# A top-k attention and a two-layer MLP on one core: where the halves, the mask's operands, the values' products and the turned weights' transfers stand

## The chip, the core and the metric

The kernel runs on one core of a Trainium2 chip. The core has a TensorE (PE, matrix products, with a queue for weight loads, PEld), a VectorE (DVE), a ScalarE (ACT), a GpSimd (POOL) and a SyncE (SP), whose queue issues nearly all transfers here. Each engine runs its own instructions in the order in which the program wrote them, and engines wait for each other through semaphores. The metric is the device time of one execution in microseconds (us); less is better.

## The reference

Attention with a hard top-k mask, followed by a block with a layer norm, two weight matrices and a residual:

```python
# q, k, v: (8 batches, 8 heads, 576 rows, 64)
scores = scale * np.matmul(q, k.transpose(0, 1, 3, 2))
kth = np.partition(scores, -32, axis=-1)[..., -32:-31]
scores = np.where(scores >= kth, scores, -1e9)
scores = scores - np.max(scores, axis=-1, keepdims=True)
attn = np.exp(scores)
attn = attn / (np.sum(attn, axis=-1, keepdims=True) + 1e-09)
attn_out = np.matmul(attn, v)
x = attn_out.transpose(0, 2, 1, 3).reshape(8, 576, 512)
xn = (x - mean(x)) / np.sqrt(var(x) + 1e-06) * g_ln
out = x + np.maximum(xn @ w_ch1, 0.0) @ w_ch2   # 512 -> 2048 -> 512
```

q, k, v and g_ln arrive as float32, and all arithmetic is float32; the two weight matrices come as 64-bit numbers, which the kernel turns into float32 itself in its first steps (`Piece`).

## The kernel before, in words

**Units, groups, jobs.** A *unit* is 128 query rows of both heads of a head pair: two score tiles of 128 x 576. The 576 rows of a batch make four such units (qt 0 to 3) and a *rest* unit, whose single tile holds the last 64 rows of both heads. A batch has four head pairs, so 20 units, and the whole run has 160. Two or three units of one head pair make a *group*, which is also a *job* here: [0, 1], [2, 3] and [rest] in batch 0, [0, 1] and [2, 3, rest] in batch 1, [0, 1, rest] and [2, 3] from batch 2 on. The four head pairs of one kind of group come one after another.

**Steps.** The main loop (L1170) goes through steps n = 0, 1, 2, ... and in each step writes the instructions of several units in different stages, so that all engines have work. In step n, apart from the first eight units:

- unit n+2: `scores` (L366): TensorE's products, copied by ScalarE into a tile `sc` (a pool of 5 buffers);
- unit n+1 (`nxt`): `halve` (L400, called at L1233, between the second and the third quarter of unit n's selection): VectorE takes the larger and the smaller of each two columns into `hi` (2 buffers) and `lo` (1 buffer);
- unit n (`u`): `select` in four parts (L415, called at L1199, L1228, L1264, L1298): VectorE finds eight largest at a time (MAX8) and strikes them out (MATCH_REPLACE8). The first eight stay in `u.top`, the last eight in `u.thr`, whose column 7 is the threshold;
- unit n-1 (`mk`): `prepare` (L442, called at L1209): GpSimd first runs `watch` (L452), which notes from `hi` whether the halving may have lost a value, then makes the two operands of the mask, `edge` and `bias`, in spare columns of `u.thr`. Later in the step `mask` (L483, called at L1254 and L1282): a Relu on ScalarE and a subtraction on GpSimd for each tile, into `e` (2 buffers). For the first 18 units (`CONVERTING`) VectorE runs `watch` and makes both operands at the end of the unit's own step (L1300);
- unit n-2 (`ex`): `weigh` (L491): ScalarE's Exp with its row sums. Then the weights have to be turned, so that keys lie along partitions, into the group's tile `pt` (1 buffer): either by TensorE and ScalarE (`turn`, L542: four transposes and one copy for each tile, and a transpose and a copy for the last columns), or, for a *moved* unit, by VectorE (`move`, L523: 32 x 32 blocks are turned in place in `sc`, the tile goes to memory in one transfer, L534, and comes back in four, L537), while the last columns still go through TensorE (`parts[-1]`, L1280). Moved are the units from batch 2 on that aren't rest units and aren't the last of their group: 72;
- the group whose last unit is n-3: `values` (L600, called at L1197): TensorE's products of V with `pt`, and one product with the tile `ends` for the last keys; `take_values` (L618), then `place` (L630) turns the result back and scales it.

**V's tile.** `load_values` (L305) brings V of a head pair by SP; it is written near the end of the step after the job's last unit (L1286). `fill_ends` (L311) copies two corners of it into the single tile `ends` on GpSimd; it is written in the middle of the next step (L1251), ahead of `mask`.

**The first eight units** (`EARLY`) run a step closer: mask and weights of unit n-1 and values of n-2 in step n, beside the conversion of the weight matrices.

**The block.** When four head pairs have given their part of two row tiles, a block of 256 rows is queued (`give`, L1121): mean and variance on VectorE, the transposes, 64 products with w_ch1 and 56 with w_ch2 (seven products of halves instead of eight, with sums on GpSimd, L818). `fill` (L263), called eight times in each step, puts a planned share of these products between the attention's instructions on TensorE, and runs the actions that were put off by a number of such calls (`Later`, L237). What is left after the last step (`END`, L1014) is run off at the end (L1317).

The kernel is written out twice; the second copy runs only where `watch` has found a doubt, and doesn't run here. In all stages SP's transfers stand in the order of the text: a transfer that waits holds up all that is written after it on SP.

Of the kernel before, what the change touches and what calls it, by code (L numbers as in the profile page):

```python
# [10 lines left out]
ALU = mybir.AluOpType  # L11
# [8 lines left out]
STEEP = 2.0**90  # L20
# [9 lines left out]
def compute(  # L30
# [229 lines left out]

    loads = Later()

    def fill(least=0):  # L263
        tick[0] += 1
        loads.settle(LOAD_AGE)
        ends_later.settle(END_AGE)
        fetch_forms(FETCH_AGE)
        owed[0] = min(owed[0] + share[0], 6.0)
        while todo and (not todo[0][3] or todo[0][3]()):
            if owed[0] < todo[0][1] / 2 and least <= 0:  # L270
                break
            least -= 1
            pop()
# [168 lines left out]
    def prepare(u):  # L442

        nt = len(u.tiles)
        u.bias, u.edge = u.thr[:, 0:nt, 5], u.thr[:, 0:nt, 6]
        if doubt is not None:
            watch(u)
        eng = nc.vector if u.i < CONVERTING else nc.gpsimd
        eng.tensor_scalar(u.edge, u.thr[:, 0:nt, 7], STEEP, 0.0, ALU.mult, ALU.add)  # L449
        eng.tensor_scalar(u.bias, u.top[:, 0:nt, 0], -scale, 0.0, ALU.mult, ALU.add)  # L450

    def watch(u):  # L452

        nt = len(u.tiles)
        c = 1 + 2 * (u.i % 16)
        eng = nc.vector if u.i < CONVERTING else nc.gpsimd
        eng.tensor_tensor(  # L457
            watched[:, c : c + nt], u.hi[:, 0:nt, HALF + 7], u.thr[:, 0:nt, 7], ALU.subtract
        )
        if u.i % 16 == 15 or u.i == N - 1:  # L460
            u.ends_watch = True
# [61 lines left out]
    def move(u):  # L523

        i0 = place_of(u)
        ni = P // 32
        blocks = u.sc[:].rearrange("p t n -> p (t n)")[:, 0 : 2 * JP]
        for t in range(2):
            nc.vector.transpose(
                blocks.rearrange("p (j t c n) -> p j t c n", j=ni, t=2, c=J)[:, :, t],  # L530
                u.e[:, t, t * R : t * R + JP].rearrange("p (c j k) -> p j c k", c=J, k=32),
            )
        hbm = hbmpool.tile([P, 2 * JP], FP32, tag="turned", name="turned")
        nc.sync.dma_start(hbm[:], blocks)  # L534
        for j in range(ni):
            to = u.group.pt[j * 32 : (j + 1) * 32, 0 : 2 * J].rearrange("k c n -> k (c n)")
            nc.sync.dma_start(  # L537
                to[:, i0 * 2 * P : (i0 + ni) * 2 * P].rearrange("k (i x) -> k i x", i=ni),
                hbm[:, j * 2 * P : (j + 1) * 2 * P].rearrange("(i k) x -> k i x", k=32),
            )  # L540

# [393 lines left out]
    PER_ROW = 1.71e-3  # L935
    SUM_AGE, END_AGE, FETCH_AGE, STORE_AGE, LOAD_AGE = 7, 6, 10, 8, 3
    blocks = []
    plain_done, formed, used, fetched = [None], [None], [], [0]
# [74 lines left out]
    N = len(units)  # L1013
    END = N + 6  # L1014

# [11 lines left out]

    for u in units[jobs[5 * NHP].first :]:
        u.moved = not u.rest and u is not u.group.units[-1]


    full = slice(0, P)
# [10 lines left out]
    for j in jobs:  # L1043
        if j.hp == NHP - 1:
            b = j.b
            step = j.last + (3 if j.last < EARLY else 4)
            tiles = [(b, qt) for g in j.groups for qt in g.qts if qt < J]
# [24 lines left out]
    def at(i):  # L1072
        return units[i] if 0 <= i < N else None

    def after(n):

        turned = at(n - 1) if n - 1 < EARLY else at(n - 2) if n - 2 >= EARLY else None
        last = at(n - 2) if n - 2 < EARLY else at(n - 3) if n - 3 >= EARLY else None
        return turned, last.group if last and last is last.group.units[-1] else None

# [89 lines left out]
    for n in range(END):  # L1170
# [12 lines left out]
        late = late if late and late.rest and late.job.b % 2 else None  # L1183
        parts = turn(ex) if ex else []
        early = ex is not None and n - 1 < EARLY
# [10 lines left out]
        if g:  # L1196
            values(g)  # L1197
        if u:
            select(u, 0)  # L1199
# [5 lines left out]
        if n == gives_first:  # L1205
            for blk, i in rows_of.pop(n):
                blk.stats(i)
        if mk and mk.i >= CONVERTING:
            prepare(mk)  # L1209
        if early:  # L1210
            for t in range(2):
                mask(ex, t)
            for t in range(2):
                weigh(ex, t)
# [6 lines left out]
        if g:  # L1221
            take_values(g)
        if parts and not moved:
            parts[0]()
# [4 lines left out]
        for x in batches.get(n - 1, []):  # L1229

            x.shift()
        if nxt:
            halve(nxt)  # L1233
        sums_later.settle(SUM_AGE)
# [13 lines left out]
        if not quick:  # L1248
            weights(n, 1)
        if n in ends_due:  # L1250
            fill_ends(ends_due.pop(n))  # L1251
        fill()
        if mk and not early:
            mask(mk, 0)  # L1254
        if g:
# [27 lines left out]
        fill()  # L1283
        for x in (u if n < EARLY else None, mk if n > EARLY else None):
            if x and x is units[x.job.last]:
                load_values(x.job)  # L1286
                ends_due[n + 1] = x.job
        if quick:
# [8 lines left out]
        if u:  # L1297
            select(u, 3)  # L1298
            if u.i < CONVERTING:
                prepare(u)  # L1300
        for x in (g, quick):
# [73 lines left out]
```

## Time and profile before

| | us |
|---|---|
| median of 3 runs | 1684.97 (1684.85 to 1687.71) |
| the profiled execution | 1683.85 |
| its span, first to last instruction | 1682.1 |
| busy: TensorE / VectorE / GpSimd / ScalarE | 1517.3 / 1339.3 / 1118.3 / 1067.6 |
| mean granted TensorE clock | 0.959 of full speed |
| products of the block with w_ch1 (L750) | 2304 instructions, two for each float32 product |
| products of the block with w_ch2 (L907, L789) | 1904 and 64 instructions |
| mask subtraction on GpSimd (L489) | 288 instructions, 1428 ns each |
| halves on VectorE (L412, L413) | 160 of each, 778 and 743 ns each |
| blocks turned by VectorE (L529) | 144 instructions, 685 ns each |

Busy time is the time in which an engine's profiled instructions run; an engine's idle time before an instruction is put down to what released it. A matmul's end is modelled, and matmuls overlap, so TensorE's busy share is an upper bound of its use.

### The profile page before, as it was taken

To read this page: it belongs to the slowest core of one execution; us is meant where nothing else is said; L and a number is where in the kernel's file an instruction comes from. 1 tells how busy PE (TensorE), PEld (TensorE's weight loads), DVE (VectorE), ACT (ScalarE), POOL (GpSimd) and SP (SyncE) were. 2 spreads that over 40 slices of the span, in tenths; PEclk is the share of its full clock that TensorE was granted. 3 is DMA by queue.
4 is the path that set the end of the run, shared out by engine and by line. 5 is a ranking of instruction groups with operands and counts; after the bars stand their busy time and mean duration, and the time that the engine had idled before them with its cause. 6 is when DMAs were issued, how large, how long until landed. Compare 5 with 4: busy or idle time off the path is not lost. (4 is left out here: it accounts for less than half of the span.)

```text
span 1682.1 us, 27351 instructions
## 1 busy us (share of the span) xinstructions
PE 1517.3 (90%) x7898; PEld 1137.5 (68%) x7898; DVE 1339.3 (80%) x3990; ACT 1067.6 (63%) x2712; POOL 1118.3 (66%) x1742
## 2 busy tenths in 40 slices
PE   3557889999979998999899999999999999999997
PEld 1335546677656676667677777677677776778886
DVE  5999988788879988899889988799889988884000
ACT  6777856677656766667566765676556765754411
POOL 4667967967556675668576866676657775757433
PEclk9768999999989999999999999999999999999999
DMA  6523334411455445544555444545555455442211
GB/s 177 151 86 129 117 75 118 119 44 46 109 150 170 116 124 146 153 143 125 161 156 160 127 136 135 157 130 134 158 147 164 123 140 167 146 129 86 85 35 52
DMA packets 355687, 211.51 MB, mean 126 GB/s; under 512 B 247492, under 2 KB 327880, under 8 KB 355528
## 3 DMA queue, kind: packets, MB, share of 16 engines
q1 hardware_dynamic: 350792, 209.08, 43.4%
q8 instruction: 65, 1.06, 0.3%
q10 hardware_dynamic: 4736, 0.59, 0.2%
q14 instruction: 94, 0.77, 0.1%
HBM read 145.62 MB, written 63.96 MB: 125 GB/s over the span
## 5 line engine op out<-in xcount | busy, mean ns | idle before, releaser
L750 PE MATMUL hps<-xT,w 128*128 128x256 f32 x2304 | 548.5, 383 | 2.4 <-ACT xT L712 2.4
L489 POOL TENSOR_TENSOR e<-e,sc 128x576 f32<-128x576 f32 x288 | 408.6, 1428 | 178.6 <-ACT e L486 149.5
L750 PEld LDWEIGHTS hps<-xT,w 128*128 128x128 f32 x2304 | 421.9, 191 | 72.9 <-issue 14.9
L434 DVE MAX8 m<-hi 128x8 f32<-128x296 f32 (+1 forms) x1152 | 458.2, 444 | 0.2
L420 DVE MATCH_REPLACE8 hi<-m,hi 128x288 f32<-128x288 f32 (+1 forms) x864 | 378.5, 444 | 0.0
L497 ACT ACTIVATE e<-e,m 128x576 f32<-128x576 f32 x288 | 225.0, 781 | 185.0 <-POOL e L489 184.6
L907 PE MATMUL ops<-w,h 128*128 128x256 f32 x1360 | 325.1, 381 | 0.0
L907 PEld LDWEIGHTS ops<-w,h 128*128 128x128 f32 x1360 | 247.6, 190 | 40.4 <-issue 7.7
L412 DVE TENSOR_TENSOR hi<-sc 128x576 f32<-128x576 f32 (+1 forms) x160 | 124.5, 778 | 183.5 <-POOL watched L457 178.4
L486 ACT ACTIVATE e<-sc,m 128x576 f32<-128x576 f32 x288 | 224.3, 782 | 13.5 <-POOL m L449 12.5
L372 ACT COPY sc<-scps 128x288 f32<-128x288 f32 x576 | 193.0, 406 | 38.0 <-PE scps L391 18.8
L605 PE MATMUL av<-pt,vb 128*64 128x256 f32 (+2 forms) x1088 | 164.4, 450 | 49.7 <-DMA qin<-in_q_dram 24.4
L314 POOL COPY ends<-vb 64x64 f32<-64x64 f32 x136 | 34.0, 250 | 219.1 <-DMA vb<-in_v_dram 180.9
L605 PEld LDWEIGHTS av<-pt,vb 128*64 128x64 f32 x1088 | 84.4, 154 | 121.0 <-issue 84.2
L773 ACT ACTIVATE h<-hps 128x512 f32<-128x512 f32 x144 | 86.5, 600 | 91.9 <-PE hps L750 90.9
L391 PE MATMUL scps<-kT,late_qT 64*128 64x288 f32 (+3 forms) x832 | 128.1, 415 | 6.2 <-ACT pt L563 5.5
L907 PE MATMUL ops<-wt,s 128*128 128x256 f32 x544 | 129.2, 381 | 0.0
L551 PE MATMUL tp<-ident,e 128*128 128x128 f32 x576 | 94.9, 291 | 38.1 <-ACT e L497 37.9
L551 PEld LDWEIGHTS tp<-ident,e 128*128 128x128 f32 x576 | 74.3, 149 | 66.5 <-ACT e L497 51.6
L413 DVE TENSOR_TENSOR lo<-sc 128x576 f32<-128x576 f32 (+1 forms) x160 | 118.9, 743 | 0.0
L391 PE MATMUL scps<-kT,qT 64*128 64x288 f32 x512 | 94.3, 469 | 26.9 <-ACT sign L167 11.8
L426 DVE MAX8 hi<-lo 128x8 f32<-128x288 f32 x288 | 118.1, 446 | 0.0
(107 smaller groups left out, 1998.4 us busy)
## 6 DMA issues: line engine op xcount, KB each, us to landing
turned<-sc SPq DMA_DIRECT2D x72, 512.0 KB, 2.6
pt<-turned SPq DMA_DIRECT2D x288, 128.0 KB, 2.8
w<-forms SPq DMA_DIRECT2D x136, 256.0 KB, 4.1
vb<-in_v_dram SPq DMA_DIRECT2D x68, 288.0 KB, 3.9
raw<-in_moe_w_ch_dram SPq DMA_DIRECT2D x32, 512.0 KB, 3.7
kT<-kept SPq DMA_DIRECT2D x36, 288.0 KB, 3.5
kin<-in_k_dram SPq DMA_DIRECT2D x128, 72.0 KB, 2.4
kept<-kT SPq DMA_DIRECT2D x32, 288.0 KB, 3.2
```

What stands on the lines that cost most here:

```text
L372: nc.scalar.copy(u.sc[:, t, s * HALF : (s + 1) * HALF], made[s][t][:, 0:HALF])
L391: nc.tensor.matmul(ps[i * R : i * R + ql, o : o + width], qT[r, q0 : q0 + ql], kT[r, k0 : k0 + width], start=True, stop=True,)
L412: nc.vector.tensor_tensor(hi, a, b, ALU.max)
L420: nc.vector.match_replace(x, m[:, t, :], x, LOWEST)
L434: nc.vector.max(m[:, t, :], u.hi[:, t, 0:width])
L486: nc.scalar.activation(u.e[:, t], u.sc[:, t], AF.Relu, bias=u.edge[:, t : t + 1], scale=-STEEP)
L489: nc.gpsimd.tensor_tensor(u.e[:, t], u.e[:, t], u.sc[:, t], ALU.subtract)
L497: nc.scalar.activation(u.e[:, t], u.e[:, t], AF.Exp, bias=u.bias[:, t : t + 1], scale=-scale, accum_out=g.den[:, col : col + 1],)
L551: nc.tensor.transpose(ps[:, c * P : (c + 1) * P], u.e[:, t, c * P + t * R : (c + 1) * P + t * R], ident[:],)
L605: nc.tensor.matmul(av[h * D : (h + 1) * D, 0 : g.nq], vb[:, h * (J + 1) + c, :], g.blocks[:, h, 0 : g.nq // 32, c, :], start=(c == 0), sto ...
L750: nc.tensor.matmul(ps[0][:, side * N : (side + 1) * N], w1[:, c, f * P : (f + 1) * P], self.xT[:, c, 0:N], start=(c == 0), stop=(c == NC - 1),
L907: nc.tensor.matmul(bank[name][:, 0:Q], a(j), rhs, start=first and j == 0, stop=(j == G - 1), skip_group_check=not first,)
```

## The change

The halves of the next unit go from the middle of the step to its end. `prepare` runs on ScalarE for all units, in place in columns of `u.top` and `u.thr`, right ahead of the mask; `watch` runs on GpSimd for all units, early in the step. A group's products with V come two, three or four steps after its last unit (`lag`): four where the next job's first unit is moved. `move` only turns the blocks in its own step; the transfer to memory is written two `fill` calls later (`SEND_AGE`), and the four transfers back, with the turn of the last columns, are written one step later, behind the products with V. Moved are now the units from the second kind of group of batch 0 on (`units[EARLY:]`), 88 in all. `load_values` and `fill_ends` change places within the step. `END` grows by one step, and so do the steps at which blocks are given behind a lag of four.

```diff
@@ fill
+        sends.settle(SEND_AGE)
         ends_later.settle(END_AGE)
@@ prepare, watch
-        u.bias, u.edge = u.thr[:, 0:nt, 5], u.thr[:, 0:nt, 6]
-        if doubt is not None:
-            watch(u)
-        eng = nc.vector if u.i < CONVERTING else nc.gpsimd
-        eng.tensor_scalar(u.edge, u.thr[:, 0:nt, 7], STEEP, 0.0, ALU.mult, ALU.add)
-        eng.tensor_scalar(u.bias, u.top[:, 0:nt, 0], -scale, 0.0, ALU.mult, ALU.add)
+        u.bias, u.edge = u.top[:, 0:nt, 0], u.thr[:, 0:nt, 7]
+        nc.scalar.mul(u.edge, u.edge, STEEP)
+        nc.scalar.mul(u.bias, u.bias, -scale)
...
-        eng = nc.vector if u.i < CONVERTING else nc.gpsimd
-        eng.tensor_tensor(
+        nc.gpsimd.tensor_tensor(
@@ move
-        nc.sync.dma_start(hbm[:], blocks)
-        for j in range(ni):
-            to = ...
-            nc.sync.dma_start(...)
+
+        def bring():
+            i0 = place_of(u)
+            for j in range(ni):
+                to = ...
+                nc.sync.dma_start(...)
+
+        sends.add(lambda: nc.sync.dma_start(hbm[:], blocks))
+        brings[u.i + 3] = bring
@@ the plan
+    SEND_AGE = 2
-    END = N + 6
+    END = N + 7
-    for u in units[jobs[5 * NHP].first :]:
+    for u in units[EARLY:]:
         u.moved = not u.rest and u is not u.group.units[-1]
+    for j, after_j in zip(jobs, jobs[1:] + [None]):
+        waits = after_j is not None and units[after_j.first].moved
+        j.groups[0].lag = 2 if j.last < EARLY else 4 if waits else 3
-            step = j.last + (3 if j.last < EARLY else 4)
+            step = j.last + 1 + j.groups[0].lag
@@ after(n): the group whose lag is reached at step n
-        last = at(n - 2) if n - 2 < EARLY else at(n - 3) if n - 3 >= EARLY else None
-        return turned, last.group if last and last is last.group.units[-1] else None
+        for age in (2, 3, 4):
+            last = at(n - age)
+            if last and last is last.group.units[-1] and last.group.lag == age:
+                return turned, last.group
+        return turned, None
@@ the step
-        parts = turn(ex) if ex else []
+        parts = turn(ex) if ex and not ex.moved else []
...
         if g:
             values(g)
+        if n in brings:
+            brings.pop(n)()
+            turn(at(n - 3))[-1]()
         if u:
             select(u, 0)
...
-        if mk and mk.i >= CONVERTING:
-            prepare(mk)
+        if mk and doubt is not None:
+            watch(mk)
         if early:
+            prepare(ex)
...
-        if nxt:
-            halve(nxt)
         sums_later.settle(SUM_AGE)
...
             weights(n, 1)
-        if n in ends_due:
-            fill_ends(ends_due.pop(n))
+        for x in (u if n < EARLY else None, mk if n > EARLY else None):
+            if x and x is units[x.job.last]:
+                load_values(x.job)
+                ends_due[n + 1] = x.job
         fill()
         if mk and not early:
+            prepare(mk)
             mask(mk, 0)
...
             mask(mk, 1)
         fill()
-        for x in (u if n < EARLY else None, mk if n > EARLY else None):
-            if x and x is units[x.job.last]:
-                load_values(x.job)
-                ends_due[n + 1] = x.job
+        if n in ends_due:
+            fill_ends(ends_due.pop(n))
...
             select(u, 3)
-            if u.i < CONVERTING:
-                prepare(u)
+        if nxt:
+            halve(nxt)
```

## The prediction

> **What bounds the kernel now.** I read the table of busy times by stretch first, with the run cut where the halve of units 20, 40, ... 140 starts and where the last unit's does: nine stages, the first with the conversion of the weights, the last (147.3 us) with no selection left. Columns: length, then busy time (and instructions) of PE, PEld, DVE, ACT and POOL, then the granted clock.
>
> ```profile
> 0.00:239.90 239.90, 154.51 (x660) 94.99 (x661) 205.57 (x547) 178.05 (x403) 166.22 (x163) 0.85 0.43 123
> 239.90:413.60 173.70, 166.47 (x948) 119.80 (x948) 148.33 (x467) 127.06 (x330) 132.51 (x203) 0.97 0.33 87
> 413.60:597.50 183.90, 164.40 (x861) 119.99 (x856) 160.82 (x487) 118.85 (x314) 117.96 (x196) 0.94 0.46 131
> 597.50:784.00 186.50, 170.08 (x906) 128.17 (x905) 164.57 (x500) 119.20 (x316) 124.20 (x205) 0.97 0.50 143
> 784.00:969.50 185.50, 179.29 (x962) 137.37 (x961) 163.51 (x493) 121.43 (x318) 130.32 (x218) 0.99 0.50 144
> 969.50:1159.20 189.70, 181.87 (x972) 138.89 (x971) 163.16 (x495) 122.61 (x327) 128.60 (x217) 0.98 0.51 145
> 1159.20:1345.70 186.50, 179.18 (x959) 136.87 (x958) 163.06 (x492) 121.13 (x315) 123.30 (x204) 0.98 0.49 142
> 1345.70:1534.80 189.10, 184.80 (x980) 143.63 (x980) 154.60 (x469) 118.80 (x306) 124.53 (x205) 0.99 0.46 134
> ```
>
> No engine is full in stages 2 to 4: TensorE and VectorE both stand some 10% of the time. In stages 5 to 8 TensorE is recorded busy 96 to 98%, but that count is generous: matmul ends are modelled. What TensorE needs I count instead. In the timeline sixteen block products in a row take 3.62 us, one ending 0.38 after its start: 0.216 us from start to start. The rest of a stage of 20 units is about 56 us: scores 20 x 1.15 (8 matmuls 1.24 us), 8 groups' products with V at 2.7 (16 take 2.37, the two with ends 0.6 to 0.8), about 112 transposes at 0.109 (four in 0.60 with one tail). Stages 5 to 8 hold 546, 548, 537 and 585 block products (L750 and L907 asked for by stretch), so need 118 + 56 = 174, 174, 172 and 180 us; stages 3 and 4 with 438 and 487 need 151 and 161; stage 2, with 364, 28 long ones at 0.43 and 194 transposes, 155. All lie below the lengths.
>
> The waits say who holds whom (total, times, longest):
>
> ```profile
> ACT e L497 <- POOL e L489: 184.6, 93, 9.4
> POOL ends L314 <- DMA vb<-in_v_dram: 180.9, 38, 11.9
> DVE hi L412 <- POOL watched L457: 178.4, 71, 11.4
> ...
> PE av L605 <- DMA qin<-in_q_dram: 24.4, 6, 5.8
> ...
> SPq L534 <- DVE m L434: 423.7, 71, 14.3
> SPq L537 <- DMA turned<-sc: 175.9, 72, 5.3
> ```
>
> The second line is the root of the first and third, as one place in the timeline shows:
>
> ```profile
> 1239.94 0.50 SPq L309 DMA_DIRECT2D vb<-in_v_dram  x1
> ...
> 1244.59 0.52 POOL L314 COPY ends<-vb 64x64 f32<-64x64 f32 x2 [7.59 <-DMA vb<-in_v_dram]
> ...
> 1244.73 2.37 PE L605 MATMUL av<-pt,vb 128*64 128x320 f32 x16 [2.90 <-issue]
> ...
> 1246.64 0.78 ACT L497 ACTIVATE e<-e,m 128x576 f32<-128x576 f32 x1 [5.62 <-POOL e L489]
> ...
> 1248.17 0.76 DVE L412 TENSOR_TENSOR hi<-sc 128x576 f32<-128x576 f32 x1 [5.93 <-POOL watched L457]
> ```
>
> V's load stands on SP behind the sending of the turned weights, which waits for VectorE, and the bringing back, which waits for the sending to land. It is issued late, GpSimd stands 7.59 us in fill_ends, and behind it in GpSimd's queue are the mask's subtraction (ScalarE's Exp waits) and the next watch, which frees the buffer that halve wants (VectorE waits 5.93).
>
> **The change, part by part.**
>
> *Load and corners of V.* The load is written half a step earlier, ahead of the next sending, the copy half a step later: some 4 us each at 9.3 us a step, against a landing of 3.9 (median). The 180.9 us on GpSimd should go, and with them most of VectorE's 178.4. Late next: fill_ends now stands behind the previous group's products with V in the same step, since `ends` is one tile; it waits if TensorE lags. Behind it are only the next watch and later sums.
>
> *Halves at the end.* No work added; the same wait gets another half step (4 us, when the waits average 178.4/71 = 2.5). Behind a halve that still waits stands the next unit's selection.
>
> *Mask operands.* GpSimd loses 143 x (518 + 428 ns) = 135 us. VectorE loses, in the first 17 units, 17 x (660 + 182 + 648 ns) = 25.3 us. ScalarE gains 320 multiplications of 2 columns; none is in the trace, the nearest row is L509 (128 x 4) with 205 ns: 65.6 us, from 1067.6 to some 1114 of 1682 after what it loses below. In stages 2 to 8 this lies in ScalarE's idle time (at least 46 us of each); without that cover it is 0.41 us a unit. The multiplications wait for watch on GpSimd, as edge did before.
>
> *Products with V four steps behind; sending and bringing in two steps.* TensorE's waits at L605 (24.4 for a transfer, 10.3 issue, 6.5, 4.1 and 2.9 for others: 48 us) should go: the turned weights have two steps instead of less than one. The bringing no longer blocks SP until the sending lands (175.9), but on SP it now waits for the earlier products with V (one pt). Behind it on SP stand the fetches of K and Q, the stores, V's load and the next sending. I cost that at nothing; the cover is a step of slack for each, and a fetch that comes late stops TensorE's scores. The e tile is held a step longer, of two; the release comes early in the step in which the next mask wants it. If that fails, ScalarE stands at the mask.
>
> *88 units instead of 72.* Sixteen more, 4 in stage 1 and 12 in stage 2: TensorE loses 128 transposes (14 us), ScalarE 32 copies at 582 ns (18.6), VectorE gains 32 turns at 685 ns (21.9: 5.5 and 16.4), SP 80 issues and the transfers 16.8 MB on 211.5 (stage 2's are busy 33%). VectorE's 16.4 lies on the path, since stage 2 then needs 148.3 + 16.4 = 165 of it against TensorE's 155 - 10.5; were TensorE the bound there, it would be a gain of 10.5 instead.
>
> **The sum**, against the profiled execution's 1683.85 us (the median, 1684.97, is 1.1 above). Stages 2 to 8 need the larger of the two engines: 165, 161, 165, 174, 174, 172, 180, together 1191; they take 1294.9. How near can they come? VectorE, when nothing held it (50 to 100 us), stood 1.4%; stage 8 with its remaining waits lies 5% over its need. I take 3%: 1227, so -68; the ends are -104 (no rest) and 0.
>
> Stage 1: VectorE's 25.3 go, 5.5 come. But there ScalarE is nearly as full: from 69.69 to 82.19 us it ran a whole early step of 12.5 us with 2.6 idle, all in its own chain of scores and mask. I take -4. The ends: -20 (all of VectorE's saving), +14 (17 units x 0.8: two multiplications and a trip to GpSimd for watch, which VectorE did before). Last stage: the program order shows 13 fewer block products written by the 151st unit's scores (1717 for 1730), two instructions each: +5.6 in the tail.
>
> 1683.85 - 68 - 4 + 5 = 1617.
>
> One rule of the Trainium skill speaks against moving the halves. Row: the halve L412 took 1138 ns on average in stage 1 and 731 in stage 7, with the same shapes; if the halves of the three stages that VectorE sets (60 x 2) all took the slow row's time, that would be 120 x 0.407 = +49 us. I take 0, since the old place, right behind watch, had GpSimd at work too. The skill's page "SBUF — State Buffer", section "SBUF: two separate sides", says that a VectorE operation with two inputs in SBUF and a GpSimd operation exclude each other for a whole instruction. By that rule a halve that meets a subtraction (1428 ns) could wait all of it, at most 120 x 1.43 = +172, and the sum would be 1789; no row here shows a wait of that size.
>
> **Rivals.**
>
> *Only TensorE's waits at V go (1650).* If TensorE's recorded busy time is its true need, stages 5 to 8 have 6.2, 7.8, 7.3 and 4.3 us to give, and what VectorE gains it waits away at the scores. The 48 us at L605 go, less some 14 (the tail's 5.6, and 8, a sixth of ScalarE's net 47 below, in which TensorE would wait for a bank): 1684 - 34. For it: 96 to 98%. Against: the count by 0.216.
>
> *The wait moves to TensorE (1680).* fill_ends waits for the products with V as long as it did for the load, and VectorE at halve behind it; of the sum only stage 1's -4 is left. For it: 9.3 us under this name before (PE av). Against: the products open their step, the copy closes it.
>
> *ScalarE becomes the pace (1706).* Its multiplications stand in its queue until watch is through, and behind them are the copies that free TensorE's product banks. Place: the middle of each step. Price: 65.6 - 18.6 = 47 net, all on the path, less VectorE's 25: +22. It decides once ScalarE's work and its chained waits fill a step. Now they don't: 6.1 of 9.3 us busy and 185/160 = 1.2 waiting. For it: stage 1, where they nearly do.
>
> *No rest at all (1581):* each stage at the need of its larger engine, -104, with the same -4 and +5; no stage before came nearer than 5%.
>
> **Chances.** Forecast 0.55 (its own range 1592 to 1645), rival one 0.20, two 0.08 (half of it faster, a quarter the same, a quarter slower), three 0.11, four 0.06. Faster by over 0.2%, about what a measurement here can tell from no change, 0.85; within 0.02; slower 0.13. The range reaches to rival one with its spread and leaves out four, three and most of two: 1590 to 1672.
>
> **What would show it.** Right: "POOL ends <- DMA vb" below 30 us, "DVE hi <- POOL watched" below 50, L605's waits below 15; stages 3 and 4 about 166 to 172 us, 5 to 8 about 177 to 185; ScalarE's multiplications near 205 ns. Wrong: a new row of over 60 us at the multiplications or at ends behind TensorE; SP's bringing holding up a fetch for which TensorE stands; stage 1 longer than 240; halves over 1 us; the granted clock below 0.95.

## The result, and the profile after

The changed kernel takes 1704.81 us in the median of four runs (1702.3 to 1707.74), the kernel before 1684.91 on the same chip: 1.0116 times as long, interval 1.0102 to 1.0131. The forecast was 1617. The profiled execution has a span of 1704.8 us, against 1682.1, and a mean granted clock of 0.940, against 0.959.

First the busy times by stretch of the changed kernel, cut like those of before where the halve of units 20, 40, ... 140 starts and where the last unit's does. Columns: length, busy time (and instructions) of PE, PEld, DVE, ACT, POOL, then the granted clock, the transfers' share and GB/s.

```profile
0.00:246.00 246.00, 159.83 (x672) 97.21 (x672) 196.81 (x515) 180.07 (x436) 167.60 (x178) 0.78 0.48 137
246.00:425.50 179.50, 152.34 (x833) 112.44 (x833) 168.23 (x484) 122.56 (x352) 125.48 (x167) 0.94 0.50 143
425.50:598.50 173.00, 154.08 (x815) 112.48 (x814) 170.09 (x493) 117.00 (x341) 107.73 (x148) 0.95 0.55 154
598.50:787.20 188.70, 174.31 (x907) 131.43 (x906) 174.78 (x500) 124.86 (x355) 113.84 (x167) 0.95 0.49 141
787.20:967.60 180.40, 179.11 (x970) 137.26 (x969) 173.36 (x493) 128.36 (x365) 121.58 (x178) 1.00 0.54 149
967.60:1167.00 199.40, 184.79 (x955) 141.29 (x954) 173.93 (x495) 125.00 (x357) 117.29 (x176) 0.95 0.49 138
1167.00:1344.40 177.40, 175.91 (x961) 135.56 (x960) 173.79 (x491) 125.88 (x356) 114.86 (x164) 1.00 0.52 149
1344.40:1541.90 197.50, 185.38 (x952) 142.95 (x951) 164.12 (x473) 123.03 (x346) 111.52 (x168) 0.97 0.43 127
1541.90:1704.80 162.90, 150.07 (x721) 128.35 (x719) 11.89 (x40) 42.63 (x100) 70.55 (x130) 0.96 0.19 61
```

The sum hides two opposite things. Stages 3, 5 and 7 are 10.9, 5.1 and 9.1 us shorter than before and run at a clock of 0.95 to 1.00. Stages 2, 4, 6 and 8 are 5.8, 2.2, 9.7 and 8.4 us longer and run at 0.94 to 0.97. The stages are the batches, one each, so something happens in every second batch. The last stretch is 15.6 us longer, the first 6.1. These two are blurred by the cut, since a halve now stands half a step later: to the start of unit 20's selection, whose place in the step stays, the first stretch takes 247.3 us against 245.5 before, and from the start of unit 159's the last takes 161.6 against 142.1. Cut in that way stages 3, 5 and 7 are still shorter and 2, 4, 6 and 8 longer.

The waits of the changed kernel (total, times, longest) name it:

```profile
POOL e L487 <- ACT e L484: 462.8, 169, 9.3
...
PE xo L656 <- POOL oTr L640: 44.7, 16, 4.0
DVE sc L526 <- ACT e L495: 35.2, 30, 2.3
DVE sc L526 <- POOL e L487: 34.4, 13, 6.2
...
PE tp L582 <- ACT sc L374: 28.9, 10, 8.6
...
DVE hi L414 <- POOL watched L455: 11.7, 6, 3.0
```

The engines' waits that the change was forecast to remove are gone: GpSimd waits for V nowhere, VectorE's 178.4 us at watch are 11.7, TensorE's at the products with V have left the list. In their place stands a row that the trace of before doesn't have: TensorE waits 16 times, 44.7 us, at L656, the transpose in `place_rest`, for GpSimd's copy of the rest columns into `oTr` (L640, in `place`). Sixteen is four odd batches times four head pairs. A second row that is new, 28.9 us at L582, is the transpose of a moved unit's last columns; it is taken up again under the open points.

SP's queue wasn't relieved as forecast. At the bringing (L536) it still stands for the sending to land, 183.6 us against 175.9 before, and a wait for TensorE's products with V has come to it, of which the trace of before has none:

```profile
SPq L536 <- DMA turned<-sc: 183.6, 80, 6.2
SPq L536 <- PE av L614: 166.5, 46, 10.4
```

One place of the sixteen at L656 in the timeline of the changed kernel (start, length, engine, line; in brackets the idle time before it and what ended it):

```profile
1058.26 2.32 PE L909 MATMUL ops<-w,h 128*128 128x256 f32 x10
...
1060.42 0.38 PE L649 MATMUL xo<-ident,oT 128*128 128x128 f32 x2
...
1060.70 0.77 ACT L484 ACTIVATE e<-sc,m 128x576 f32<-128x576 f32 x1
...
1061.55 1.86 POOL L487 TENSOR_TENSOR e<-e,sc 128x576 f32<-128x576 f32 x1 [3.38 <-ACT e L484]
...
1062.08 1.95 DVE L415 TENSOR_TENSOR lo<-sc 128x576 f32<-128x576 f32 x1
...
1063.36 0.76 POOL L640 COPY oTr<-oT 128x64 f32<-128x64 f32 x1
...
1064.18 0.33 PE L656 MATMUL xo<-ident,oTr 128*128 128x128 f32 x1 [3.37 <-POOL oTr L640]
...
1064.34 4.87 PE L909 MATMUL ops<-w,h 128*128 128x256 f32 x14
```

`place` transposes full tiles on TensorE and copies the rest columns on GpSimd. The copy stands in GpSimd's queue behind the mask's subtraction, which waits for ScalarE's Relu, so it comes 3 us after TensorE is ready; and `place_rest`, which wants the whole of `oTr`, is the next thing on TensorE. Before, `place` ran three steps after the group's last unit and `place_rest` four steps after it (`late = at(n - 4)`), so a step lay between. The change put `place`, with its products, four steps behind where the next unit is moved, and left `late` alone: both now fall in one step.

The timeline also shows what follows. Ten block products took 2.32 us before the stand, 14 take 4.87 after it. The clock column of two short stretches of the same trace, before and after:

```profile
1058.20:1060.50 2.30, 2.30 (x13) 2.00 (x12) 2.30 (x8) 1.86 (x7) 0.00 (x0) 1.00 0.36 109
1064.40:1068.80 4.40, 4.40 (x14) 3.59 (x14) 4.40 (x17) 0.52 (x2) 3.18 (x8) 0.61 0.75 273
```

After a stand of 3.37 us TensorE is granted 0.61 of its clock for the next 4.4 us, so the stand is paid for again.

The halves (full tiles, by shape) and ScalarE's multiplications after:

```profile
L415 DVE TENSOR_TENSOR lo<-sc 128x576 f32<-128x576 f32 x128 | 139.3, 1089 | 0.0
L414 DVE TENSOR_TENSOR hi<-sc 128x576 f32<-128x576 f32 x128 | 132.6, 1036 | 16.7 <-POOL watched L455 11.7 <-ACT sc L374 5.0
...
L448 ACT ACTIVATE m<-m 128x2 f32<-128x2 f32 x128 | 27.3, 213 | 21.2 <-POOL watched L455 21.2
```

The halves took 830 and 794 ns before. With the smaller shapes VectorE spends 306.8 us on them, 63 more than before. Row L415 of the timeline is one that took 1.95 us while a subtraction ran.

### The profile page after: what moved, and what is told of

The parts are those of the page before. It is cut to its first block, busy times and chain, and to the rows that moved or that the text cites. A ratio compares the mean times of both kernels' runs of the same rounds, so it can differ in the third digit from the quotient of the medians.

```text
span 1704.8 us, 27056 instructions
## 1 busy us (share of the span) xinstructions
PE 1515.8 (89%) x7770; PEld 1139.0 (67%) x7770; DVE 1407.0 (83%) x3971; ACT 1089.4 (64%) x3000; POOL 1050.5 (62%) x1473
## 4 chain that ended last, share of the span: by engine, by line
PE 65%; POOL 15%; ACT 9%; DVE 8%; issue 2%; DMA 1%; SPq 0%; ACTq 0%; POOLq 0%; DVEq 0%
PE hps L752 24%; PE ops L909 21%; PE scps L393 8%; POOL e L487 6%; PE av L607 5%; DVE m L436 2%; PE tp L553 2%; DVE hi L422 2%; POOL w L181 2%; PE av L614 2%; ACT e L484 1%; ACT e L495 1%; POOL wt L179 1%; ACT sc L374 1%; PE tp L711 1%
## 5 line engine op out<-in xcount | busy, mean ns | idle before, releaser
L487 POOL TENSOR_TENSOR e<-e,sc 128x576 f32<-128x576 f32 x288 | 431.4, 1506 | 471.6 <-ACT e L484 462.8
L752 PEld LDWEIGHTS hps<-xT,w 128*128 128x128 f32 x2304 | 436.7, 196 | 71.7 <-issue 11.1
L909 PEld LDWEIGHTS ops<-w,h 128*128 128x128 f32 x1360 | 262.8, 200 | 44.4 <-issue 4.2
L526 DVE STREAM_TRANSPOSE sc<-e 128x512 f32<-128x512 f32 x176 | 117.4, 691 | 85.7 <-ACT e L495 35.2
L414 DVE TENSOR_TENSOR hi<-sc 128x576 f32<-128x576 f32 (+1 forms) x160 | 149.7, 936 | 16.7 <-POOL watched L455 11.7
L415 DVE TENSOR_TENSOR lo<-sc 128x576 f32<-128x576 f32 (+1 forms) x160 | 157.1, 982 | 0.0
L607 PE MATMUL av<-pt,vb 128*64 128x256 f32 (+2 forms) x1088 | 145.6, 411 | 0.0
L607 PEld LDWEIGHTS av<-pt,vb 128*64 128x64 f32 x1088 | 72.9, 141 | 58.5 <-issue 14.0
L909 PEld LDWEIGHTS ops<-wt,s 128*128 128x128 f32 x544 | 100.9, 193 | 15.5 <-issue 2.3
L553 PE MATMUL tp<-ident,e 128*128 128x128 f32 x448 | 76.5, 299 | 37.2 <-ACT e L495 34.8
```

The lines of the kernel that those rows point to most:

```text
L414: nc.vector.tensor_tensor(hi, a, b, ALU.max)
L415: nc.vector.tensor_tensor(lo, a, b, ALU.min)
L487: nc.gpsimd.tensor_tensor(u.e[:, t], u.e[:, t], u.sc[:, t], ALU.subtract)
L607: nc.tensor.matmul(av[h * D : (h + 1) * D, 0 : g.nq], vb[:, h * (J + 1) + c, :], g.blocks[:, h, 0 : g.nq // 32, c, :], start=(c == 0), sto ...
L752: nc.tensor.matmul(ps[0][:, side * N : (side + 1) * N], w1[:, c, f * P : (f + 1) * P], self.xT[:, c, 0:N], start=(c == 0), stop=(c == NC - 1),
L909: nc.tensor.matmul(bank[name][:, 0:Q], a(j), rhs, start=first and j == 0, stop=(j == G - 1), skip_group_check=not first,)
```

## The experiments

Fifteen kernels, each against the kernel before on the same chip. TensorE's stand is the span less PE's busy time in the same profile.

| kernel | built on | ratio to before (interval) | span, us | TensorE stands, us |
|---|---|---|---|---|
| before | | 1 | 1682.1 | 164.8 |
| after | | 1.0116 (1.0102 to 1.0131) | 1704.8 | 189.0 |
| e1 place_rest a step later | after | 0.9772 (0.9752 to 0.9791) | 1645.1 | 154.6 |
| e2 products with V three steps behind | after | 0.9735 (0.9715 to 0.9756) | 1636.1 | 153.1 |
| e3 halves in the middle | after | 1.0057 (1.0038 to 1.0076) | 1690.9 | 193.1 |
| e4 load and corners of V exchanged | before | 0.9719 (0.9698 to 0.9741) | 1637.0 | 135.7 |
| e5 place_rest a step earlier | before | 1.0308 (1.0275 to 1.0341) | 1732.5 | 197.0 |
| e6 halves in the middle | e2 | 0.9721 (0.9704 to 0.9738) | 1644.3 | 155.2 |
| e7 72 units | e2 | 0.9698 (0.9676 to 0.9719) | 1639.2 | 140.8 |
| e8 mask operands as before | e2 | 0.9728 (0.9709 to 0.9747) | 1637.0 | 153.5 |
| e9 rest columns copied by ScalarE | after | 0.9883 (0.9857 to 0.9908) | 1666.8 | 172.1 |
| e10 halves in the middle, 72 units | e2 | 0.9646 (0.9619 to 0.9673) | 1634.3 | 134.5 |
| e11 load of V alone | before | 0.9647 (0.9617 to 0.9678) | 1625.2 | 125.8 |
| e12 corners of V alone | before | 0.9959 (0.9943 to 0.9974) | 1682.9 | 165.7 |
| e13 corners back in the middle | e2 | 0.9628 (0.9602 to 0.9655) | 1621.2 | 142.4 |
| e14 corners back in the middle | e10 | 0.9633 (0.9614 to 0.9652) | 1626.8 | 129.7 |
| e15 load and corners as before | e1 | 0.9804 (0.9785 to 0.9822) | 1649.0 | 158.1 |

### The meeting of place and place_rest: e1, e2, e5, e9

e1 takes the two apart by moving the second:

```diff
-        late = at(n - 4)
+        late = at(n - 5)
```

> The changed kernel with place_rest one step later (rest unit of n-5 instead of n-4). Theory A (place_rest now stands right behind place, whose copy into oTr GpSimd makes late): the 44.7 us that TensorE waited at xo for oTr go, and with them most half-clock stretches and VectorE's waits at the turn in the stages of odd batches; 1704.8 falls to 1650-1675, the stages of odd batches by 6 to 12 us each, the others stay. Theory B (the halves at the step's end collide with GpSimd's subtraction, VectorE +63 us busy): 1690-1700. Theory C (ScalarE with 66 us more work sets the pace): 1700 or more.

e2 by moving the first back:

```diff
-        j.groups[0].lag = 2 if j.last < EARLY else 4 if waits else 3
+        j.groups[0].lag = 2 if j.last < EARLY else 3
```

> The changed kernel with the products with V three steps behind everywhere but in the first eight units. Theory A: place and place_rest stand a step apart again, the wait at oTr goes, 1660-1680. If the fourth step is what took TensorE's waits at the products with V away (48 us before, 0 after), they come back here and the time stays near 1700.

Each turns the loss into a gain, of 2.3 and 2.7%, a little more than theory A forecast. In e2 TensorE's waits at the products with V are 15.6 us in all, against 49.7 before: most of them stay away with three steps too, so it isn't the fourth step that removes them. In e1 the wait at L656 has left the trace, and the stages of the odd batches lose their excess; its stages 4, 6 and 8, with the same columns as above:

```profile
596.40:770.60 174.20, 166.93 (x912) 126.65 (x911) 172.88 (x500) 125.22 (x361) 116.47 (x167) 1.00 0.55 154
...
949.80:1125.30 175.50, 175.37 (x957) 135.52 (x956) 172.64 (x495) 124.66 (x360) 116.57 (x176) 1.00 0.57 158
...
1302.20:1483.20 181.00, 177.50 (x952) 138.56 (x951) 167.62 (x472) 122.45 (x346) 113.15 (x168) 1.00 0.47 138
```

(The second stage isn't mended: 181.9 us in e1, where the products stay four steps behind; 177.5 in e2.) The three are 14.5, 23.9 and 16.5 us shorter than in the changed kernel: 54.9 of the 59.7 us between the spans. TensorE's stand differs by 34.4; the lower clock of these three stages (0.05 of 188.7, 0.05 of 199.4, 0.03 of 197.5) makes about 25 more, an estimate from these rows. The halves still take 941 and 976 ns on average (936 and 982 in the changed kernel), so they aren't the cause of the loss.

e5 does the opposite to the kernel before, and nothing else (the sums that `place_rest` divides by are made a step earlier too):

```diff
-        late = at(n - 4)
+        late = at(n - 3)
...
-        last_rest = at(n - 3)
+        last_rest = at(n - 2)
```

> The kernel before, with only the transposes of the last tiles' outputs (place_rest) one step earlier, so that they stand right behind place in the same step, as they do in the changed kernel. Theory A (this meeting is what cost the changed kernel its gain): TensorE's wait at the transposes for GpSimd's copy of oTr appears, some 30 to 50 us in 16 places, the stages of the odd batches get longer by 4 to 10 us each, and the time goes up by 20 to 50 us (1.2 to 3 per cent). Rival (the meeting only costs because the changed kernel's GpSimd and TensorE are closer to full): the row appears, but the time stays within 0.5 per cent of before.

It is 3.1% slower, a little over the top of theory A's range. The row appears in its waits, and stages 4 and 6 take 199.9 and 206.4 us where before they took 186.5 and 189.7:

```profile
PE xo L654 <- POOL oTr L638: 34.5, 16, 3.8
```

```profile
609.70:809.60 199.90, 174.89 (x906) 131.13 (x905) 164.28 (x499) 119.99 (x316) 125.94 (x205) 0.95 0.47 134
995.70:1202.10 206.40, 187.37 (x957) 141.56 (x955) 162.78 (x496) 121.83 (x320) 128.03 (x213) 0.94 0.47 134
```

So the meeting costs in either kernel, and with e1 and e2 that it is the cause of the loss is shown. e9 asks whether it is GpSimd's queue:

```diff
-                nc.gpsimd.tensor_copy(
+                nc.scalar.copy(
                     oTr[hp][:, r0 : r0 + R], g.oT[:, i * P : i * P + R]
```

> The changed kernel, products with V four steps behind and place_rest still right behind place; only the copy of the rest columns to oTr is made by ScalarE instead of GpSimd. Theory A1 (TensorE waits because the copy stands in GpSimd's queue behind a mask subtraction of 1.5 us): the wait of TensorE for oTr falls from 44.7 to below 15 us and the time to that of e1, 0.975 to 0.983. Rival A2 (any copy in between is late, because both are in the same step): the wait goes over to ScalarE's copy with 30 us or more, and the time stays at 1.005 or above.

Neither theory fits. The wait goes over to ScalarE but is smaller:

```profile
PE xo L656 <- ACT oTr L640: 26.2, 16, 2.3
```

The longest is 2.3 us instead of 4.0, and the time lies between the two forecasts, at 0.9883. Two thirds of the loss (0.0233 of the 0.0344 between after and e1) go with GpSimd's queue; the rest stays with the copy on ScalarE and its reader still in one step.

### What the late load of V cost before: e4, e11, e12, e15

e4 is the change's exchange of `load_values` and `fill_ends` alone, in the kernel before; e11 moves only the load, e12 only the corners:

```diff
         if n in ends_due:
             fill_ends(ends_due.pop(n))
+        for x in (u if n < EARLY else None, mk if n > EARLY else None):
+            if x and x is units[x.job.last]:
+                load_values(x.job)
+                ends_due[n + 1] = x.job
...
-        for x in (u if n < EARLY else None, mk if n > EARLY else None):
-            if x and x is units[x.job.last]:
-                load_values(x.job)
-                ends_due[n + 1] = x.job
```

(That is e11; in e12 the first two lines go to where the last four stand; e4 does both.)

> The kernel before, with only load_values and fill_ends exchanged in the step, as the change has them. Prediction's root cause (V's load stands behind the turned weights on SP and holds up GpSimd, which holds up the halves): GpSimd's wait for V's load falls from 181 us to under 30, VectorE's wait for watch from 178 to under 70, time 1640-1665. If TensorE is the bound as its busy share says: the waits go and the time stays within 10 us of 1684.

> The kernel before with V's load alone half a step earlier, ahead of the next sending on SP; the copy of the corners (fill_ends) stays in the middle of the next step. Theory (the load was late because it stood behind the sending of the turned weights): GpSimd's wait for vb falls from 180.9 to below 40 us and the time to 0.970 to 0.980, as with both moved. Rival (half a step is too little for one of them alone): the wait stays above 80, the time between 0.98 and 0.995.

> The kernel before with the copy of V's corners (fill_ends) alone half a step later; the load stays where it was. Theory (the load comes so late that half a step does not cover all of it): GpSimd's wait for vb falls to between 40 and 110 us, time 0.978 to 0.992. Rival (the copy's early place alone was at fault): wait below 30 us and 0.970 to 0.977.

e4 gains 2.8%, the load alone 3.5%, the corners alone 0.4%. In e4 GpSimd's wait for V is gone, as expected, but VectorE's at watch is still 113.1 us, where under 70 was expected. The waits of e12 are the instructive ones:

```profile
DVE hi L412 <- POOL watched L457: 160.5, 75, 12.0
...
ACT e L497 <- POOL e L489: 47.2, 44, 3.6
...
POOL ends L314 <- DMA vb<-in_v_dram: 35.0, 12, 6.0
PE av L605 <- DMA qin<-in_q_dram: 33.9, 7, 6.6
...
PE av L612 <- POOL ends L314: 16.4, 9, 4.0
```

Neither expectation held. GpSimd's wait for V falls from 180.9 to 35.0 us and ScalarE's at Exp from 184.6 to 47.2, and the time falls by 0.4%. So most of these waits were slack, but not necessarily all: the late copy brings a wait of its own, the last row above, and its late place costs 0.7 to 1.1% (below). The waits that went may thus have been worth 1.1 to 1.5%, an estimate from these ratios. TensorE's waits at the products with V stay, 50.4 us in all at L605 against 49.7 before, and its stand is the same within 1 us. In e11, better than expected, GpSimd doesn't wait for V at all, TensorE's waits at L605 are 15.2 us in all, and the stand is 125.8: of the 39.0 us less of standing, 34.5 are at this line. e15 tries the reverse: V late for GpSimd, but in time for TensorE, whose products stand four steps behind.

> e1 with V's load and the copy of its corners where the kernel before had them; the products with V stay four steps behind, so that TensorE has a step more before it needs V, and GpSimd has not. Theory C (what the late load cost before was TensorE's standing at the products, and GpSimd's and VectorE's waits were mostly slack, as e12 suggests): GpSimd's wait for vb is back with 100 us or more, the time stays at 0.972 to 0.985. Rival (the prediction's root: GpSimd's wait holds Exp and halve, and these set the pace): vb back with 100 us or more and the time at 0.992 or above.

GpSimd's wait comes back with 62.2 us only, below the 100 that both expected, and the time is 0.3% above e1's, which the two intervals don't tell apart; theory C's range held. With a third of the wait back this is no full test. What V's late load cost was for the greater part TensorE's standing; how much of the 3.5% went by way of GpSimd isn't shown, and the estimate above puts it at 1.1 to 1.5%.

e11 against e4 and e13 against e2 also price the corners' late copy: 0.7 and 1.1%. In e2 TensorE waits for it at the last of the products:

```profile
PE av L614 <- POOL ends L316: 21.0, 12, 3.6
```

In the changed kernel, with its products a step later, this wait is 1.2 us.

### The small parts: e3, e6, e7, e8

e3 and e6 put the halves back:

```diff
             x.shift()
+        if nxt:
+            halve(nxt)
         sums_later.settle(SUM_AGE)
...
-        if nxt:
-            halve(nxt)
```

> The changed kernel with the halves of the next unit back in the middle of the step. Theory B: a halve takes 0.75 us instead of 0.94 and 0.98, VectorE's busy time falls by 50-60 us, the stages of even batches by 5 to 8 us each, time 1670-1690. Theory A alone: the stages of odd batches stay as they are, time within 8 us of 1704.8. If the earlier place brings the wait for watch back (178 us before the change), the time rises above 1710.

> e2 (the changed kernel, products with V three steps behind throughout) with the halves back in the middle of the step. Theory B (at the end of the step the halves meet GpSimd's subtractions, and the 60 us that VectorE loses by it lie on the path): the halves fall from 935 to about 850 ns, the wait at watch returns (100 to 140 us), and the time falls by 0.5 to 1.5 per cent against e2 (1619 to 1635). Rival (the two prices cancel, or VectorE has room for both): within 0.3 per cent of e2's 0.9735. Second rival (the place at the end is a gain, because it takes the wait at watch away): slower than e2 by 0.5 per cent or more.

With the meeting in place (e3) the middle is 0.6% better, without it (e6) the two are equal, as the first rival had it. In e6 the halves of full tiles take 954 and 907 ns instead of 1014 and 1024, and VectorE's wait at watch is 96.5 us instead of 16.6: one price for the other. The first stage, cut at unit 20's halve, is 240.6 us in e6 (239.3 in e3) against 244.9 in e2, but that cut moves with the halves. To the start of unit 20's selection it is the same in e2 and e6 (before, changed kernel, e2 and e6 in turn):

```profile
0.00:245.50 245.50, 160.11 (x697) 98.08 (x698) 211.07 (x560) 181.85 (x413) 168.03 (x167) 0.85 0.43 121
...
0.00:247.30 247.30, 161.13 (x677) 97.99 (x678) 198.11 (x516) 180.73 (x438) 167.60 (x178) 0.79 0.48 136
...
0.00:246.30 246.30, 159.85 (x679) 97.27 (x680) 197.25 (x517) 181.29 (x440) 167.59 (x178) 0.79 0.49 137
...
0.00:246.20 246.20, 162.58 (x687) 99.14 (x689) 189.28 (x516) 182.86 (x444) 164.16 (x179) 0.80 0.50 139
```

e7 takes the sixteen units back from VectorE, e8 the mask's operands from ScalarE:

```diff
-    for u in units[EARLY:]:
+    for u in units[jobs[5 * NHP].first :]:
```

> e2 with 72 instead of 88 units turned by VectorE: the sixteen units of stage 1 and 2 are turned by TensorE again. Theory (VectorE's 32 turns lay on stage 2's path, as the prediction put it): stage 2 shorter by 8 to 16 us, from 177.5 to some 162 to 169, time 0.9735 less 0.5 to 1 per cent. Rival (stage 2 is not VectorE's, TensorE's transposes and ScalarE's copies cost as much): stage 2 within 4 us, time within 0.3 per cent of e2's.

> e2 with the mask operands as before: VectorE for the first units, GpSimd after them, nothing of it on ScalarE. Theory (ScalarE's multiplications are hidden in stages 2 to 8, and in stage 1 they stand in its chain, which costs what VectorE saves): stage 1 shorter by 3 to 6 us (from 244.9 to about 240), stages 2 to 8 within 10 us in sum, time within 0.4 per cent of e2. Rival (the multiplications stand ahead of copies that TensorE and GpSimd wait for, so they cost in every stage): faster than e2 by 1 per cent or more. Second rival (GpSimd needs the 135 us that it is rid of): slower than e2 by 0.5 per cent or more.

In e7 stage 2 takes 173.3 us instead of 177.5, not the 162 to 169 of the theory, and stage 3 takes 178.7 instead of 173.4: what the second stage gains the third gives back, and the intervals of the two ratios don't tell the times apart. e8 is the same as e2 to 0.1%, as its theory had it, but the first stage isn't shorter: 244.7 us against 244.9. So it is worth nothing either way whether ScalarE's multiplications or the old operations make the operands.

### Mended versions: e10, e13, e14

> e2 with the halves back in the middle and 72 units turned by VectorE: what is left of the change is mask operands on ScalarE, V's load and corners half a step moved, sending and bringing in two steps. Theory (each part is worth nothing by itself, TensorE sets stages 5 to 8 at some 177 us): 0.967 to 0.974, stages 5 to 8 at 175 to 179, the last of them at 187 to 190. Rival (the two partly good places add up): below 0.966, 1632 or less.

> e2 with the copy of V's corners back in the middle of the step (V's load stays early). Theory (late in the step the copy holds TensorE at the last of the products with V, 21.0 us in e2, and that is on the path, as e4 against e11 suggests): the wait of TensorE for ends falls below 8 us and the time to 0.963 to 0.969. Rival (e2's 0.9735 is set by the halves and not by the corners): within 0.3 per cent of 0.9735.

> e10 with the copy of V's corners in the middle: of the change only V's early load, the mask operands on ScalarE and the sending and bringing in two steps are left. Theory (the copy's place is worth what it was between e4 and e11, 0.7 per cent): 0.955 to 0.961, below both e10 and e11. Rival (TensorE's work sets some 1628 us, whatever is mended): 0.962 to 0.967.

e13 is the changed kernel with two places mended: products three steps behind (e2's line) and the corners back in the middle,

```diff
             if x and x is units[x.job.last]:
                 load_values(x.job)
                 ends_due[n + 1] = x.job
...
-        if n in ends_due:
-            fill_ends(ends_due.pop(n))
```

with the last two lines written ahead of the load. It takes 1625.32 us against 1691.13, a little better than expected, and the wait for the corners is gone from its trace. Its stages 4 to 8:

```profile
589.60:764.50 174.90, 167.63 (x917) 128.36 (x918) 171.74 (x499) 125.06 (x361) 119.66 (x172) 1.00 0.54 151
764.50:940.10 175.60, 174.69 (x952) 134.67 (x949) 172.32 (x493) 123.38 (x353) 120.72 (x174) 1.00 0.55 152
940.10:1118.40 178.30, 176.83 (x970) 137.06 (x969) 173.46 (x496) 127.24 (x365) 115.36 (x171) 1.00 0.55 154
1118.40:1293.70 175.30, 173.84 (x947) 134.18 (x946) 169.69 (x492) 125.23 (x354) 111.08 (x164) 1.00 0.55 155
1293.70:1479.80 186.10, 185.32 (x992) 144.56 (x991) 164.42 (x473) 120.99 (x340) 117.47 (x178) 1.00 0.45 131
```

The clock is full in all of them and TensorE is recorded busy to within 2 us from stage 5 on. e10 was better than its theory, and its rival held: next to e2 it gains 0.9%, more than e6 and e7 found for its two parts (0.1 and 0.4%), and why isn't shown. But e14, with the halves and the 88 units undone as well as the corners, is no better than e13, as its rival had it, and e11, which is the kernel before with one transfer written half a step earlier, stands beside both (0.9647). Some 1625 to 1629 us is the level that these three share, and one moved load reaches it.

## Why the prediction was wrong

*The failed step* is that on the products with V. It expected the 48 us at L605 to go, and what the fourth step brings with it it costed "at nothing", with SP's queue and `e` as the things to look at. It followed the products, the bringing and the transfers, but not `place`, which goes with the products, nor `place_rest`, which is timed from the rest unit by an index of its own and didn't move. Of the sum, this term was missing: after against e1, 59.7 us of span, of the 89 by which the profiled stretches missed their forecast (68.9 in stages 2 to 8, the rest in the first stage and the tail). None of the rivals held it. The second let GpSimd wait at `ends` for TensorE's products, of which the changed kernel's trace has no row; the wait that came runs the other way, TensorE for GpSimd. The third gave 1706, nearly the measured time, by another road: e1 and e2 have all of ScalarE's multiplications and lie at 0.977 and 0.974, so its number was right by chance.

*The root and what hung on it.* That V's load was late, and that SP's order made it so, held: e11. That its cost ran through GpSimd, Exp and halve didn't, for the greater part: e12 takes most of the first two waits away for 0.4%, or 1.1 to 1.5% without the price of its late copy. Nor did most of VectorE's 178.4 us at watch hang on V: 101.6 are left in e11 and 113.1 in e4, where GpSimd doesn't wait for V, and 139.6 in e3, the changed kernel with the halves in the middle. It is the halves' new place that makes them 11.7. The cost of the late load ran mostly through TensorE. The forecast read the biggest rows of the waits; the 24.4 us at L605, far smaller, belonged to the engine that set the pace.

*Stages 2 to 8.* The forecast was 1227 us for them together. Changed, they take 1295.9; mended, in e13, 174.9 + 170.3 + 174.9 + 175.6 + 178.3 + 175.3 + 186.1 = 1235.4. So the need by the larger engine with 3% on top was a fair measure of what the stages can do, once nothing else is put in their way. That e13 ends at 1625, so near 1617, is in part luck: its stages 2 to 8 are 8.4 us over the forecast, and its tail, 139.7 us from the start of the last unit's selection against 142.1 before, is 8.0 under it. The forecast also had SP freed of the wait for the sending to land; that wait is still there, with no harm at the products with V.

*Stage 1*: forecast -4, measured +6.1, but +1.8 to the start of unit 20's selection, so that most of the +6.1 is the cut. What failed there is VectorE's saving as a gain in time. To that point its busy time falls by 13.0 us instead of 20, because the halves grew; with the halves in the middle (e6) it falls by 21.8, and e2 and e6 still take the same, 246.3 and 246.2 us. ScalarE's multiplications were neither the gain nor the loss of that term (e8). What sets the length of this stage isn't shown.

*The tail*: forecast +5.6, measured +15.6, or +19.5 from the start of unit 159's selection. Products with V four steps behind give the last blocks a step later: in the last stretch e1 has 721 TensorE instructions and 161.9 us, e2, three steps behind, 644 and 141.3.

*Halves at the end*: the row's bound was +49 for 120 of the halves and VectorE's own work grew by 63 over all 320, yet without the meeting the time as a whole doesn't show it (e6). The Trainium skill's page "SBUF — State Buffer", section "SBUF: two separate sides", names the mechanism, a VectorE operation with two inputs and a GpSimd operation that shut each other out, and the 1.95 us of L415 beside a subtraction of 1.86 agree with it. Its bound of 172 us was not reached.

*Mask operands*: 213 ns and 205 ns measured, 205 forecast, hidden as costed (e8). What sending and bringing in two steps is worth was not tried by itself. *88 units*: VectorE's 16.4 us in stage 2 were put on the path; e7 shows 4.2 there, given back in stage 3.

Of the signs listed, the three on waits that should go came true, and of the stages' lengths those of 5 and 7. So did those of a wrong forecast: stage 1 over 240 us (by a cut that moved with the halves), halves over 1 us (full tiles), a clock below 0.95. No sign covered a wait that was new at a line the prediction hadn't named.

Open: why e1 is 1.4% slower than e13. Its trace shows TensorE waiting 31.2 us at L582 behind ScalarE's copies of the scores, which e13 doesn't have, SP standing 141.9 us for the products with V before it brings (L536), of which e13 has nothing, a second stage 7.0 us longer, and the longer tail; these weren't tried apart. Nor was it tried what sets the 1625 us.

## What to carry to other kernels

When a piece of work is moved by a step, list everything that is called with it and everything that is timed by another index but reads its results; check on each queue whether a producer and its reader now meet in one step. Compare stages between points that the change doesn't move. And price waits by the engine that sets the pace, not by their size: taking 146 us of waiting off GpSimd came with 0.4%, or 1.1 to 1.5% by the estimate above; a load moved by half a step, which took 34.5 us off TensorE's waits at one line, gave 3.5%.

## What was unexpected in the hardware

A microsecond in which TensorE stands goes with more than one of time. Of the kernels with 72 turned units, the slowest and the fastest, e5 and e11, differ by 71.2 us of standing and 107.3 of span, 1.5 to 1; of those with 88, after and e13, by 46.6 and 83.6, 1.8 to 1. The clock makes up much of it: 0.61 for 4.4 us after a stand of 3.37, and, by the estimate above, about 25 of the 59.7 us between after and e1.

The sixteen stands at L656 of the changed kernel show what length of stand goes with a lower clock. The twelve in stages 4, 6 and 8 lasted 2.39 to 4.05 us, and in the six microseconds after each the clock is 0.50 to 0.76. Of the four in stage 2, the three of 2.13 us are followed by a clock of 1.00, the one of 2.40 by 0.72. Two of these stretches, after a stand of 2.13 us and after the one of 2.39:

```profile
410.87:416.87 6.00, 6.00 (x33) 4.72 (x34) 6.00 (x19) 3.60 (x11) 2.44 (x4) 1.00 0.70 147
...
1409.55:1415.55 6.00, 6.00 (x22) 4.67 (x24) 6.00 (x22) 1.86 (x6) 2.13 (x4) 0.72 0.66 227
```

The Trainium skill's page "TensorE: Matmul & The Clock Gate", Part 1 on the clock gate, puts both the idle time that lowers the clock and the busy time that raises it again at about 3.4 us. The second fits: half the clock for 3.4 of 4.4 us makes the 0.61 above, an estimate with the page's figures. The first doesn't: here the lower clock follows stands of 2.4 us as well, and the measurement decides.
